# Moving two score pieces, their transposes and the U sums of each later batch in a fused attention and mixer kernel

## The chip, the cores and the metric

The kernel runs on one core of one Trainium2 chip. Its time is the device time of one execution in microseconds; before the change the median of three runs is 314.85 us (314.42 to 315.06). A core has a matrix engine (TensorE, PE), a vector engine (VectorE, DVE), a scalar engine (ScalarE, ACT), a general engine (GpSimd, POOL) and a sync engine (SyncE, SP). Each runs its own list of instructions in order; semaphores tie the lists together. DMA queues move data between HBM and the on-chip memory.

## The reference

Sliding window attention over 8 batches of 8 heads, 576 positions and head size 64, followed by a mixer: a low rank mix over positions (U and V, rank 32) with a residual, then two dense layers with a relu and a residual.

```python
scores = scale * np.matmul(q, k.transpose(0, 1, 3, 2))
rel = pos[:, None] - pos[None, :]
mask = (rel >= 0) & (rel < 64)
scores = np.where(mask, scores, -1000000000.0)
attn = softmax(scores)
x = np.matmul(attn, v)                  # heads side by side: (8, 576, 512)
h = x.transpose(0, 2, 1) @ U @ V        # mixes the 576 positions, rank 32
u = x + h.transpose(0, 2, 1)
ch = np.maximum(u @ w_ch1, 0.0) @ w_ch2 # 512 -> 2048 -> 512
out = u + ch
```

The line with softmax stands for the subtraction of the maximum, the exponential and the division by the sum.

## The kernel before

The 4608 rows (8 batches of 576) pass through the dense layers in nine chunks of 512. The loop over c at L927 writes one chunk: 32 slots with a last one for what is left, and in each slot four big matmuls. Slots 0 to 15 make psA from w1b and uT (L749), a block of 128 hidden units each, and a relu on ACT (L760) or DVE (L758, the numbers in DVE_RELU) writes it to c1. Slots 16 to 31 make psU from c1 and w2b (L793), four slots for each of four row tiles, and DVE adds u to it and sends it out (L808, L811). psA and psU share a pool of three PSUM buffers ("mm"). Two larger buffers ("big") serve scores, values and the V sums; one more bank ("tp") serves two small uses, the last head's values (xr8, L477) and a piece of the V sums (psv0, L549).

While chunk c runs, the attention of batch b = c + 1 is fitted into its slots. The order is written out by hand: the tables PLACE (batches 3 to 7), PLACE_1 and PLACE_2 give for each piece the slot after whose matmuls it is issued. Every engine receives its instructions in that order; there is no scheduler that moves them later. The pieces of a batch are:

- KT (L238): the transposes of k and q on DVE (L253), eight of them, k and q by turns. One of them reads all 128 partitions of the raw k or q and writes a quarter of kt or qt. kt and qt exist once, the raw tiles twice (by the parity of the batch).
- S (L353): five score pieces. PE writes sc (L378), ACT takes the exponential into pts (L386), DVE multiplies by the mask (L393). Piece n covers blocks 8n to 8n + 7 of 36, nine blocks to a pair of heads, so that the first two pieces need the first four transposes. pts exists once.
- VC (L140): two copies on DVE (L143, L144) that lay the values out a second time in vB.
- PV (L473, PVH at L450): the values, on PE; DVE divides by the sums and writes xs and xh.
- U (L517): the sums with U, pshh (L529), which ACT copies to hh (L538).
- V (L543): the sums with V, psv (L562), from hh.
- ADD (L572) and TR (L682): DVE adds xs to psv and so makes u (un), and transposes it into a staging tile stg.
- gather (L705): 16 small DMAs from the queues of SP, ACT and POOL that bring the staging tile into uT, the input of the next chunk.

The transposes of batch b + 1 are fitted into chunk c too, in the slots of KT_LATE. The loads of k and q (L117, four of each, each for 32 partitions) come from the POOL queue: in chunk c, one slot after the slot of V plus the gather, next_loads (L694) copies two elements of the gathered uT on POOL (hold, L698) and then issues the loads of batch c + 3. The values of batch b + 1 are loaded at the start of chunk c (L129, L135). Batches 2 and 3 are loaded earlier, in chunk 0.

Of the kernel before, what the change touches and what calls it, by code (L numbers as in the profile page):

```python
# [12 lines left out]
FP32 = mybir.dt.float32  # L13
# [3 lines left out]
def kernel(  # L17
# [12 lines left out]
    B, H, S, D = q.shape  # L30
# [3 lines left out]
    P = nc.NUM_PARTITIONS  # L34
# [12 lines left out]
    CH = 512  # L47
# [3 lines left out]
    HD = DM // 2  # L51
# [15 lines left out]
    ps_big = ctx.enter_context(tc.tile_pool(name="ps_big", bufs=2, space=bass.MemoryType.PSUM))  # L67
    first = ExitStack()
    psum = {
        "x0": first.enter_context(tc.tile_pool(name="ps_x0", bufs=2, space=bass.MemoryType.PSUM)),  # L70
    }
# [30 lines left out]
    def load_kq(b):  # L102
        r = RUN[b]
        for part in range(NJ if PAIRED[b] else 4):
            for x, src in (("k", k), ("q", q)):
                dst = raw[x, b % 2]
                if PAIRED[b]:
                    nc.gpsimd.dma_start(
                        out=dst[:, part * RD : (part + 1) * RD],
                        in_=src[b, part * NQ : (part + 1) * NQ].rearrange(  # L110
                            "i (p c) d -> (i p) (c d)", c=RP
                        ),
                    )
                    continue
                m, dh = divmod(part, 2)
                off = 32 * (1 - dh)
                nc.gpsimd.dma_start(  # L117
                    out=dst[32 * part : 32 * (part + 1), off : off + NJJ * RD].rearrange(
                        "p (n x) -> p n x", x=r * D
                    ),  # L120
                    in_=src[b, m * NJJ : (m + 1) * NJJ].rearrange(
                        "h (m p e) d -> p (h m) (e d)", p=32, e=r
                    ),
                )

    def load_v(b, first=True, second=True):
        va, vb = vA[b % 2], vB[b % 2]
        for t in range(0 if first else 2, NFULL if second else 2):
            nc.gpsimd.dma_start(  # L129
                out=va[:, t, :, 0:D],  # L130
                in_=v[b, :, t * P : (t + 1) * P, :].rearrange("h p d -> p h d"),
            )
        if not second:
            return
        nc.gpsimd.dma_start(  # L135
            out=vb[0:W, NFULL, :, 0:D],
            in_=v[b, :, NFULL * P : S, :].rearrange("h p d -> p h d"),
        )
# [90 lines left out]
    def attention(b, alone=False):  # L229
# [283 lines left out]
        hh = hh_of.setdefault(b, {})  # L513
# [3 lines left out]
        def UM(ts):  # L517
            def f():
                if ts[0] == 0:
                    big = ps_big.tile([P, 2, CH], FP32, name="pshh", tag="big")  # L520
                    hh["ps"] = big[:, 0, 0:HD]
                ps = hh["ps"]
                tops = (ub[0][:, NT - 1, :], ubh[0][:]) if not odd else (ubh[1][:], ub[1][:, 0, :])
                for t in [t for t in full if t in ts] + [t for t in ts if t == half_t]:
                    xt = (xh[odd] if t == half_t else x[:, t]).rearrange("p h d -> p (h d)")
                    n_th = 0 if t == half_t else full.index(t)
                    for n in range(2):
                        g = 2 * n + n_th % 2
                        nc.tensor.matmul(  # L529
                            ps[g * R : (g + 1) * R, :],  # L530
                            tops[n] if t == half_t else ub[odd][:, t, :],
                            xt if t == half_t else xt[:, n * HD : (n + 1) * HD],
                            start=(t != half_t and n_th < 2),
                            stop=(t == half_t or n_th == NFULL - 1),
                        )
                if ts[-1] == NT - 1:
                    hh["sb"] = wk_pool.tile([P, HD], BF16, name="hh", tag="hh")
                    nc.scalar.copy(out=hh["sb"][:], in_=ps)  # L538
            return f
# [135 lines left out]
        return pcs  # L675


    DVE_RELU = (1, 4, 7, 10, 13)
    stages = {}
    last_pieces = {}  # L680

    def TR(g):  # L682
        def f():
            c, t = divmod(g, TPC)
            if c not in stages:
                stages[c] = stg_pool.tile([P, 4 * NDC, TPC, 32], BF16, name="stg")
            nc.vector.transpose(  # L687
                out=stages[c][:, :, t, :],
                in_=u_tiles[g].rearrange("p (j x) -> p j x", x=32),
            )  # L690

        return f

    def next_loads(c):  # L694
        def f():
            for i, j in last_pieces[c + 1]:
                rows = slice(32 * j, 32 * (j + 1))
                nc.gpsimd.tensor_copy(  # L698
                    out=hold[rows, 0:1], in_=uT_of(c + 1)[rows, 0, i * TPC * 32 : i * TPC * 32 + 1]
                )  # L700
            load_kq(c + 3)

        return f
# [21 lines left out]
    def mlp(c):  # L725
# [11 lines left out]
        def ch1(i):  # L737
            def f():
# [17 lines left out]
                c1[i] = c1_pool.tile([P, CH], BF16, name=f"c1_{i}")  # L756
                if i in (DVE_RELU if c > 1 else (7, 10, 13) if c else (1, 5, 14)):
                    nc.vector.tensor_relu(out=c1[i][:], in_=ps)  # L758
# [59 lines left out]


    PLACE = {  # L820
        "VC": [2],
        "S": [0, 0, 4, 4, 9],
        "PV": [9, 12, 12],
        "KT": [14, 15, 16, 19, 21, 23, 25, 27],
        "U": [15],
        "V": [17],
    }
    PLACE_1 = {
# [13 lines left out]
        "S": [3, 3, 6, 6, 9, 9],  # L842
        "VC": [7],
        "PV": [12, 14, 14],
        "U": [17],
        "V": [18],
    }
    KT_LATE = {b: [21, 22, 23, 24, 25, 27, 28, 30] for b in range(2, B - 1)}


    def turn_over(n, cols=CH, to=None):
# [15 lines left out]
    att = {0: attention(0, alone=True)}  # L867
# [59 lines left out]
    for c in range(NCH):  # L927
        slots = [[] for _ in range(NSLOT + 1)]

        def place(b, parts, where):  # L930
            if b not in att:
                att[b] = attention(b)
            for part in parts:
                for f, s in zip(att[b][part], where[part]):
                    slots[s].append(f)

        b = c + 1
        if b == 1:
            slots[4].append(att[0]["V"][0])
            for f, n in zip(att[0]["ADD"], (5, 6, 7, 8, 4)):  # L940
                slots[n].append(f)
        if b < B:
            if b == 1:
                load_kq(2)
            if b + 1 < B:
                load_v(b + 1)
            if b == 1:
                slots[23].append(lambda: load_kq(3))
            where = {1: PLACE_1, 2: PLACE_2}.get(b, PLACE)
            if b == 2:  # L950
                place(1, ("V", "ADD"), {"V": where["V1"][:1], "ADD": where["ADD1"][:4]})
            if b == 1:
                place(1, ("KT",), where)
            if b == 2:
                att[2]["KT"] = att[2]["KT"][2:]
                place(2, ("KT",), where)
            place(b, ("VC", "S", "PV"), where)
            if b == 2:
                slots[where["V1"][1]].append(att[1]["V"][1])
                slots[where["ADD1"][4]].append(att[1]["ADD"][4])  # L960
            if b == 1:
                place(2, ("KT",), {"KT": PLACE_2["KT0"]})
            if 3 <= b + 1 < B:
                place(b + 1, ("KT",), {"KT": KT_LATE[b]} if b in KT_LATE else PLACE)
            place(b, ("U", "XT", "UP") if b == 1 else ("U", "V"), where)
        if 2 <= c + 1 < NCH:
            g0 = (b * S) // P
            first = (c + 1) * TPC
            own = [first + t - g0 for t in range(TPC) if b < B and first + t >= g0]
            at = where["V"][0] if b < B else 18  # L970
            for t in range(TPC - len(own)):
                slots[at - 1].append(TR(first + t))
            for n, t in enumerate(own):
                slots[at + n // 2].append(att[b]["ADD"][t])
                slots[at + n // 2].append(TR(g0 + t))
            ready = at
            slots[ready + 1].append(gather(c + 1))
            for n, t in enumerate(t for t in range(NT) if b < B and t not in own):
                slots[ready + 1 + n].append(att[b]["ADD"][t])
            if c > 0 and c + 3 < B:  # L980
                slots[ready + 1].append(next_loads(c))
        for n, (fill, extra) in enumerate(zip(mlp(c) + [lambda: None], slots)):
            early = c == 0 and n > 20
            for f in extra + [fill] if early else [fill] + extra:
                f()
# [30 lines left out]
```

## Time and profile before

| | |
|---|---|
| median of three runs | 314.85 us |
| profiled execution, its own time | 316.53 us |
| its span, from first to last instruction | 314.8 us |
| mean granted TensorE clock | 0.989 |
| chunk 4, from first psA to first psA | 159.46 to 191.65 us, 32.19 us |
| chunks 7 and 8, without attention | psA 13.81 us, psU 13.81 us for 64 matmuls each |
| k and q loads of a batch | eight of 288 KB read, median 10.9 and 12.0 us to landing |
| DMA packets under 512 B | 98544 of 109121 |

The page gives busy time by engine, the same in 40 slices of the span, the chain of work that ended last, and the costliest groups of instructions. The views asked of the trace beside it are the chain in order of time, the timeline of one engine, the instructions of one tile with the time that their DMAs took to land, and the busy time by stretches. A slice is 7.87 us; a digit is the busy share in tenths.

### The profile page before, as it was taken

How to read it: one execution, taken by the hardware profiler on the slowest of the kernel's cores; microseconds unless marked ns; L12 is line 12 of the kernel's file. 1: busy time of each engine (PE TensorE's matmuls, PEld its weight loads, DVE VectorE, ACT ScalarE, POOL GpSimd, SP SyncE). 2: the span in 40 equal slices, each digit the busy share in tenths (PEclk: the TensorE clock that was granted, in tenths of full speed). 3: DMA queues.
4: the chain of work that ended last, by engine and by line, in shares of the span. 5: the costliest groups of instructions: out<-in, count | busy, mean ns of one | idle time of the engine just before them, and what ended most of it. 6: DMA issues, size and time to landing. Idle time of an engine off the chain costs nothing.

```text
span 314.8 us, 7156 instructions
## 1 busy us (share of the span) xinstructions
PE 306.6 (97%) x2959; PEld 150.7 (48%) x2959; DVE 205.5 (65%) x371; ACT 105.7 (34%) x173; POOL 109.1 (35%) x162
## 2 busy tenths in 40 slices
PE   8799999998999999999999999999999999999995
PEld 7454455454444544454444444544444444444444
DVE  6655863897798679767966796689668622413111
ACT  1444752484107410551056204630463014103400
POOL 8591466482049404740583039303000300300000
PEclk9969999999999999999999999999999999999999
DMA  6999999999959995999599959995100510230011
GB/s 115 158 158 211 192 181 196 104 154 230 68 133 169 175 101 134 161 176 109 135 177 177 91 127 147 195 112 134 70 2 2 130 70 0 59 109 34 3 67 67
DMA packets 109121, 38.06 MB, mean 121 GB/s; under 512 B 98544, under 2 KB 102000, under 8 KB 109088
## 3 DMA queue, kind: packets, MB, share of 16 engines
q0 software_dynamic: 92672, 25.64, 113.6%
q1 hardware_dynamic: 11232, 10.69, 10.8%
q10 hardware_dynamic: 5184, 1.28, 2.2%
q8 instruction: 23, 0.38, 0.6%
q14 instruction: 10, 0.08, 0.1%
HBM read 48.96 MB, written 9.44 MB: 185 GB/s over the span
## 4 chain that ended last, share of the span: by engine, by line
PE 87%; DMA 6%; DVE 3%; ACT 2%; issue 1%; POOL 0%; DVEq 0%; POOLq 0%
PE psA L749 38%; PE psU L793 36%; PE sc L378 3%; DMA vB<-in_v_dram 3%; DMA qr<-in_q_dram 3%; PE xr L485 2%; PE psv L562 1%; PE psU L773 1%; PE pshh L529 1%; PE xr L417 1%; ACT pts L386 1%; DVE qt L245 1%; PE xT L626 1%; ACT pts L336 0%; PE xrh L457 0%
## 5 line engine op out<-in xcount | busy, mean ns | idle before, releaser
L749 PE MATMUL psA<-uTc,w1b 128*128 128x512 bf16 x576 | 131.0, 380 | 0.0
L793 PE MATMUL psU<-w2b,c 128*128 128x512 bf16 x560 | 125.0, 380 | 0.0
L760 ACT ACTIVATE c<-psA 128x512 bf16<-128x512 f32 x103 | 61.0, 599 | 161.8 <-PE psA L749 148.2
L749 PEld LDWEIGHTS <-w1b 128*128 128x128 bf16 x576 | 54.0, 98 | 63.6 <-issue 1.5
L793 PEld LDWEIGHTS <-c 128*128 128x128 bf16 x560 | 53.2, 98 | 64.8 <-issue 3.3
L713 POOL DMA_DIRECT2D uTc<-stg x35 | 19.2, 558 | 101.5 <-DVE stg L687 30.3
L758 DVE TENSOR_SCALAR c<-psA 128x512 bf16<-128x512 f32 x41 | 28.2, 687 | 19.8 <-PE psA L749 18.0
L808 DVE TENSOR_TENSOR osb<-psU,un 128x512 f32<-128x512 f32 x33 | 22.3, 675 | 28.7 <-PE psU L793 28.5
L393 DVE TENSOR_TENSOR pts<-pts,mask 128x1024 bf16<-128x1024 bf16 (+2 forms) x37 | 23.8, 654 | 24.4 <-ACT pts L386 23.6
L129 POOL DMA_DIRECT2D vA<-in_v_dram x32 | 28.8, 902 | 25.3 <-PE psA L749 12.4
L386 ACT ACTIVATE pts<-sc 128x1024 bf16<-128x1024 f32 (+2 forms) x37 | 31.5, 895 | 5.6 <-PE sc L378 5.6
L580 DVE TENSOR_TENSOR un<-psv,xs 128x512 bf16<-128x512 f32 x29 | 19.0, 675 | 4.7 <-PE psv L562 4.6
L687 DVE STREAM_TRANSPOSE stg<-un 128x512 bf16<-128x512 bf16 x28 | 18.8, 695 | 0.4
L117 POOL DMA_DIRECT2D kr<-in_k_dram x20 | 16.4, 820 | 5.3 <-DMA vA<-in_v_dram 2.7
L117 POOL DMA_DIRECT2D qr<-in_q_dram x20 | 16.5, 827 | 2.8 <-DMA vA<-in_v_dram 2.2
L253 DVE STREAM_TRANSPOSE kt<-kr 128x576 bf16<-128x576 bf16 x20 | 15.8, 788 | 0.1
L253 DVE STREAM_TRANSPOSE qt<-qr 128x576 bf16<-128x576 bf16 x20 | 15.7, 783 | 0.0
L378 PEld LDWEIGHTS <-kt 64*64 64x64 bf16 (+1 forms) x720 | 10.3, 106 | 10.0 <-issue 9.6
L378 PE MATMUL sc<-qt,kt 64*64 64x128 bf16 (+4 forms) x720 | 13.3, 215 | 0.9 <-issue 0.7
L499 DVE TENSOR_TENSOR xs<-xr,rcp 128x896 bf16<-128x896 f32 x12 | 13.1, 1092 | 0.1
L593 DVE TENSOR_TENSOR un<-psv,xh 64x256 bf16<-64x256 f32 x16 | 6.7, 417 | 6.7 <-PE psv L562 6.5
L853 PE MATMUL unread<-idle 128*128 128x64 bf16 (+2 forms) x108 | 7.5, 244 | 1.3 <-DVE idle L147 1.3
(93 smaller groups left out, 195.1 us busy)
## 6 DMA issues: line engine op xcount, KB each, us to landing
out_dram<-osb SPq DMA_DIRECT2D x35, 256.0 KB, 2.2
kr<-in_k_dram POOLq DMA_DIRECT2D x26, 288.0 KB, 10.9
qr<-in_q_dram POOLq DMA_DIRECT2D x26, 288.0 KB, 12.0
vA<-in_v_dram POOLq DMA_DIRECT2D x32, 128.0 KB, 12.6
w2b<-in_moe_w_ch_dram POOLq DMA_DIRECT2D x4, 512.0 KB, 12.6
uTc<-stg SPq DMA_DIRECT2D x42, 32.0 KB, 2.3
uTc<-stg ACTq DMA_DIRECT2D x35, 32.0 KB, 2.3
uTc<-stg POOLq DMA_DIRECT2D x35, 32.0 KB, 2.1
```

The costliest lines, as they stand in the source:

```text
L117: nc.gpsimd.dma_start(out=dst[32 * part : 32 * (part + 1), off : off + NJJ * RD].rearrange("p (n x) -> p n x", x=r * D), in_=src[b, m * NJ ...
L129: nc.gpsimd.dma_start(out=va[:, t, :, 0:D], in_=v[b, :, t * P : (t + 1) * P, :].rearrange("h p d -> p h d"),)
L253: nc.vector.transpose(out=dst[:, n * S : (n + 1) * S].rearrange("q (m p e) -> q m e p", p=32, e=r), in_=src[:, 32 + n * RD : 32 + (n + 1) ...
L378: nc.tensor.matmul(sc[half * W : (half + 1) * W, g, (a - lo) * W : (z - lo) * W], operand("k", g, jj, e, kb * W, (kb + 1) * W), operand("q ...
L386: nc.scalar.activation(out=dst, in_=sc[:, :, 0 : (hi - lo) * W].rearrange("p g (n w) -> p g n w", w=W), func=ACT.Exp, scale=scale,)
L393: nc.vector.tensor_tensor(out=dst, in0=dst, in1=mask[:, m0 : m0 + hi - lo, :] .unsqueeze(1) .to_broadcast([P, 2, hi - lo, W]), op=ALU.mult,)
L713: queues[n % 3].dma_start(out=uT_of(c)[32 * j : 32 * (j + 1), :, i * run : (i + 1) * run], in_=stages[c][32 * i : 32 * (i + 1)].rearrange( ...
L749: nc.tensor.matmul(to if c < 2 else to.rearrange("p (t i q) -> p t i q", i=4, t=TPC), w1b[:, dc, n * P : (n + 1) * P], uT_cols(dc), start= ...
L758: nc.vector.tensor_relu(out=c1[i][:], in_=ps)
L760: nc.scalar.activation(out=c1[i][:], in_=ps, func=ACT.Relu)
L793: nc.tensor.matmul(acc[t][:], c1[i][:, t * P : (t + 1) * P], w2b[:, i, :], start=(i == 0), stop=(i == NFC - 1),)
L808: nc.vector.tensor_tensor(out=osb[:], in0=acc[t][:], in1=u_tiles[g][:], op=ALU.add)
```

## The change

The first two score pieces of batches 3 to 7 are issued a chunk sooner, after the U sums of the preceding batch and in their slot; the other three pieces, the values and the U sums move to earlier slots. For the early pieces, the first four transposes of batches 4 to 7 move to slots 9 to 12 and those of batch 3 to slots 15 to 17; the other four follow from slot 21 on (25 for batch 3). The second layout of the values (VC) moves to slot 31 of the chunk before. The U sums of batches 2 to 7 take the bank "tp" in place of a "big" buffer. In chunk 1 the U sums of batch 2 stand at slot 19 and not 17, its V sums at slot 22 and not 18, and with them the gather and the loads that follow. Three of the five relus on DVE change their number. No instruction is added or removed.

```diff
--- before.py
+++ after.py
@@ -517,8 +517,10 @@
         def UM(ts):
             def f():
                 if ts[0] == 0:
-                    big = ps_big.tile([P, 2, CH], FP32, name="pshh", tag="big")
-                    hh["ps"] = big[:, 0, 0:HD]
+                    if b < 2:
+                        hh["ps"] = ps_big.tile([P, 2, CH], FP32, name="pshh", tag="big")[:, 0, 0:HD]
+                    else:
+                        hh["ps"] = psum["tp"].tile([P, CH], FP32, name="pshh", tag="tp")[:, 0:HD]
                 ps = hh["ps"]
                 tops = (ub[0][:, NT - 1, :], ubh[0][:]) if not odd else (ubh[1][:], ub[1][:, 0, :])
                 for t in [t for t in full if t in ts] + [t for t in ts if t == half_t]:
@@ -675,7 +677,7 @@
         return pcs
 
 
-    DVE_RELU = (1, 4, 7, 10, 13)
+    DVE_RELU = (1, 2, 5, 10, 13)
     stages = {}
     last_pieces = {}
 
@@ -818,11 +820,9 @@
 
 
     PLACE = {
-        "VC": [2],
-        "S": [0, 0, 4, 4, 9],
-        "PV": [9, 12, 12],
-        "KT": [14, 15, 16, 19, 21, 23, 25, 27],
-        "U": [15],
+        "S": [0, 0, 4],
+        "PV": [4, 7, 7],
+        "U": [14],
         "V": [17],
     }
     PLACE_1 = {
@@ -842,10 +842,13 @@
         "S": [3, 3, 6, 6, 9, 9],
         "VC": [7],
         "PV": [12, 14, 14],
-        "U": [17],
-        "V": [18],
+        "U": [19],
+        "V": [22],
     }
-    KT_LATE = {b: [21, 22, 23, 24, 25, 27, 28, 30] for b in range(2, B - 1)}
+    KT_EARLY = {b: [9, 10, 11, 12] for b in range(4, B)}
+    KT_EARLY[3] = [15, 15, 16, 17]
+    KT_LATE = {b: [21, 23, 25, 27] for b in range(4, B)}
+    KT_LATE[3] = [25, 27, 29, 30]
 
 
     def turn_over(n, cols=CH, to=None):
@@ -954,15 +957,20 @@
             if b == 2:
                 att[2]["KT"] = att[2]["KT"][2:]
                 place(2, ("KT",), where)
-            place(b, ("VC", "S", "PV"), where)
+            if b >= 3:
+                att[b]["S"] = att[b]["S"][2:]
+            place(b, ("S", "PV") if b >= 3 else ("VC", "S", "PV"), where)
             if b == 2:
                 slots[where["V1"][1]].append(att[1]["V"][1])
                 slots[where["ADD1"][4]].append(att[1]["ADD"][4])
             if b == 1:
                 place(2, ("KT",), {"KT": PLACE_2["KT0"]})
             if 3 <= b + 1 < B:
-                place(b + 1, ("KT",), {"KT": KT_LATE[b]} if b in KT_LATE else PLACE)
+                place(b + 1, ("KT",), {"KT": KT_EARLY[b + 1] + KT_LATE[b + 1]})
+                place(b + 1, ("VC",), {"VC": [31]})
             place(b, ("U", "XT", "UP") if b == 1 else ("U", "V"), where)
+            if 3 <= b + 1 < B:
+                place(b + 1, ("S",), {"S": where["U"] * 2})
         if 2 <= c + 1 < NCH:
             g0 = (b * S) // P
             first = (c + 1) * TPC
```

## The prediction

> **What bounds the kernel now.** I read the busy shares first, then the chain of waits, and last the timelines of the DVE and POOL around one batch. The page shows a TensorE that hardly pauses:
>
> ```profile
> PE 306.6 (97%) x2959; PEld 150.7 (48%) x2959; DVE 205.5 (65%) x371; ACT 105.7 (34%) x173; POOL 109.1 (35%) x162
> PE   8799999998999999999999999999999999999995
> PEclk9969999999999999999999999999999999999999
> DMA  6999999999959995999599959995100510230011
> ```
>
> The DMA row matters as much: until slice 28 the queues are full, apart from one dip per batch. The chain of waits confirms PE, and gives the cost of each piece in one steady chunk (start us, length, what):
>
> ```profile
> 159.46 0.86 PE psA L749 x4
> 160.32 0.57 PE sc L378 x32
> 160.89 3.61 PE psA L749 x16
> ...
> 173.84 2.70 PE psA L749 x12
> 176.53 0.43 PE pshh L529 x10
> 176.97 1.83 PE psU L793 x8
> 178.80 0.65 PE psv L562 x10
> 179.45 12.19 PE psU L793 x56
> 191.65 0.86 PE psA L749 x4
> ```
>
> Start to start this chunk (c=4) takes 191.65 - 159.46 = 32.19 us; one slot, four matmuls, is 0.86. The PE does the same work after the change, so a gain can only come from gaps, and there are few. What can go wrong is a wait, so I looked at what the moved pieces wait for. In the POOL timeline of chunk 2's end the loads of batch 5's k and q follow the gather of the next uT and the "hold" copies that read it; in the DVE timeline its transposes come in chunk 3:
>
> ```profile
> 124.81 0.42 POOL L698 COPY hold<-uTc 32x1 bf16<-32x1 bf16 x2 [2.39 <-DMA uTc<-stg]
> 125.40 0.83 POOL L117 DMA_DIRECT2D kr<-in_k_dram  x1 [0.17 <-issue]
> 131.03 0.83 POOL L117 DMA_DIRECT2D qr<-in_q_dram  x1
> ```
>
> ```profile
> 152.29 0.82 DVE L253 STREAM_TRANSPOSE kt<-kr 128x576 bf16<-128x576 bf16 x1
> 153.02 0.77 DVE L253 STREAM_TRANSPOSE qt<-qr 128x576 bf16<-128x576 bf16 x1
> ```
>
> The view by tile, cut to 124-132 us, gives for the four q loads (least, median, most):
>
> ```profile
> DMA to landing us min/median/max: 9.8/13.4/16.4
> ```
>
> 16.4 is the last one's, so batch 5's q is whole at 131.03 + 16.4 = 147.4. Each transpose (L253) reads all 128 partitions, and one load fills only 32 of them: every transpose, the first too, needs all four loads. Chunk 3 starts at 127.27; q lands 20.2 us into it, 4.9 us before its first transpose now.
>
> [...] So a transpose that waits holds up every relu behind it. The trace agrees in that DVE's order is the program's. [...] The windows view of the start agrees (us, then busy us of PE, PEld, DVE, ACT, POOL, granted clock, DMA, GB/s):
>
> ```profile
> 8.02:11.43 3.41, 2.79 (x61) 1.77 (x60) 1.62 (x2) 1.51 (x2) 2.44 (x4) 1.00 1.88 168
> 11.43:14.84 3.41, 2.08 (x126) 1.73 (x124) 3.17 (x7) 1.38 (x2) 1.46 (x3) 1.00 2.30 138
> 14.84:18.25 3.41, 3.09 (x42) 1.85 (x42) 1.66 (x5) 2.15 (x6) 2.52 (x5) 0.50 1.30 136
> 18.25:21.67 3.42, 3.42 (x43) 1.80 (x43) 2.37 (x6) 1.25 (x7) 3.42 (x7) 0.50 1.16 170
> ```
>
> A stretch of 3.41 us with PE busy for 2.08 was followed by two at half clock; one with 2.79 was not. [...] The trace agrees: twelve matmuls between two switches take 2.70, against 13.81/64 x 12 = 2.59 in the unbroken stretches at the end, so 0.11 per group.
>
> **The change part by part.**
>
> Small things first. The relus: five stay on DVE, other numbers; 0.69 on DVE against 0.60 on ACT, all beside matmuls: 0. The U sums in the "tp" bank: its last user, xr8, is read by slot 7, and the next, psv0, comes three slots after the 0.37 us copy of hh: 0. The V copies (0.68 + 0.70) at slot 31 of the chunk before: their last load is issued at 142.56, lands after a median 9.7, 152.3, before slot 31 (about 158): 0, and if late they would hold a DVE that has only an output sum to do. The two early score pieces keep their cost of 0.57 but ride behind the U sums, so a group disappears per batch: -0.11 five times, and the last attention chunk is 0.57 shorter, paid a chunk sooner.
>
> The transposes carry the price. The first four (k, q, k, q) of batches 4 to 7 move from slots 21-24 to 9-12 of the same chunk; the loads don't move forward. In the new order DVE has, after slot 9: k transpose, relu 10, q, k, q, relu 13, then the two masks. The psA pool has three buffers: with relu 10 held, PE stops at the matmuls of slot 13, about 13 x 0.86 + 2.2 of scores and values = 13.4 us into the chunk; with the q transposes held, the scores at slot 14 stop. Landing is at 17.4 to 20.2 us. ACT's exp and hh copy are queued behind PE, and the loads of the next batch behind this chunk's values (V, slot 17), so the delay comes again each chunk.
>
> So I follow one loop, from the V matmuls (psv) of a chunk to those of the next: psv to first k issue; first k issue to last q landing; then three transposes (0.7 + 0.7 + 0.77 = 2.2), two score pieces 0.57, three slots 2.70, together 5.47. Measured now:
> batch 4: psv 82.75, issue 94.27, q whole 99.90 + 14.5 = 114.4, so 11.52 + 20.13;
> batch 5: psv 114.15, 125.40, 147.4: 11.25 + 22.03;
> batch 6: 146.61, 155.98, 161.64 + 15.2 = 176.84: 9.37 + 20.86;
> batch 7: 178.80, 189.09, 194.72 + 15.8 = 210.52: 10.29 + 21.43.
>
> Chunk 1 first. Batch 3's last q load (issued 64.55, 18.3 to land) is whole at 82.85, its k at 80.34. Transposes now stand at slots 15-17, so the fourth ends at 85.05; PE has done slot 19 and the U sums (79.62 + 3.45 + 0.43) at 83.5 and waits 1.55. Scores 0.57 and three slots 2.70: psv at 88.35, where it was 82.75. The gather moves along (V at slot 22, not 18): uT lands 10.6 after psv, 99.0, but only 8.4 us of PE work follow, so chunk 2 starts 2.2 late; that lies inside the next wait.
>
> Then psv of chunk 2: 88.35 + 31.65 + 5.47 = 125.47; chunk 3: + 33.28 + 5.47 = 164.22; chunk 4: + 30.23 + 5.47 = 199.92; chunk 5: + 31.72 + 5.47 = 237.11. Before it was 210.99: +26.1, and less 0.68 in chunk 6: +25.4. The loops are 37.1, 38.8, 35.7, 37.2 us against 32.2 of PE work: PE idles 3.5 to 6.5 us in each.
>
> Unknown is the clock after such a stop. By the windows above, more than 1.33 us idle in one of them can halve it; each of the four stops would. [...] Half of that is lost, less 0.65 that PE would have waited for q anyway: 1.05 to 2.75, I take 1.9. What is slow behind psv costs nothing: PE waits for loads there. Below zero it can't go; at zero the masks and uT transposes behind the late scores would cost up to 1.0 in its place. Four times 1.9 is 7.6.
>
> Sum: 25.4 + 7.6 = +33.0 on the span of 314.8: 347.8, and 1.7 around it in the profiled execution (316.53). The median of the runs, 314.85, lies 1.7 below that execution; 314.85 + 33.0 = 347.9, taken as 348.
>
> **Rivals.** (a) The same loop with the clock full: +25.4, and up to 1.0 for three of the DVE's late masks, about 341. For it: stretches with small matmuls may be judged otherwise than these. Against: the start's half-clock stretch. (b) The late load is paid once: if the later loads ran ahead of PE, only chunk 2's share (125.47 - 114.15 = 11.3) would stay: 326. Against: the hold copies that tie the loads to uT. (c) The half clock lasts over the whole way from resumption to psv, about 6 us of work each time: 25.4 + 4 x 5.4 = +47, 362. (d) No stop: were q whole by 13.4 us into a chunk, the price of the transposes would be 0 and the saved switches (5 x 0.11) and chunk 2's small stop (its chunk is 32.54, not 32.19) would show: -0.9, 313.9. It decides only if landing shrinks by 4.0 us or more; the four measured landings span 1.9.
>
> **How the numbers follow.** Forecast 0.64; (a) 0.17; (b) 0.07; (c) 0.08; (d) 0.04. Landing may differ by a microsecond in each of four loops, and the clock by 0.85 each, so the forecast's own range is 341 to 355; (a) and part of (c) widen it to 334 to 358. No change means within 0.2%, what a measurement of this kernel can tell. (d) splits into faster 0.03 and same 0.01; the rest, 0.96, is slower.
>
> **What would show it.** DVE timeline: a gap before the k transpose in chunks 2 to 5, ended by kr or qr; PE gaps before psA of slot 13 and sc of slot 14; chunks of 36 to 40 us; PEclk of 0.5 after each. Were the gaps at uT or psv, or the transposes on time, the loop is wrong.

## The result and the profile after

The changed kernel takes 344.99 us (median of four runs, 344.35 to 347.11) against 314.73 for the kernel before on the same chip: a ratio of 1.0973 with a 95% interval of 1.0922 to 1.1024. (Single executions that the chip disturbed are left out, here and below; where a run gives one time only, that is why.) The profiled execution took 344.48 us, its span is 342.8 us, 28.0 more than before.

The first lines to compare are the same four of the page:

```profile
PE 312.7 (91%) x2930; PEld 154.4 (45%) x2959; DVE 205.3 (60%) x371; ACT 107.4 (31%) x173; POOL 110.6 (32%) x162
...
PE   8779999999979599995999799986999999999995
...
PEclk9999999999989879998999989998999999999999
DMA  7999999999299905999399907999510050051012
```

PE no longer runs through: there are dips four to five slices (a chunk) apart, the granted clock dips with them, and the DMA row, which was full, now has empty slices. The work is the same, so neither engine has more to do; both stand still by turns. The chain of waits says who waits for whom. This is chunk 2's end and chunk 3 (start us, length, what):

```profile
135.66 0.18 POOL hold L700
135.84 0.17 issue
136.01 0.83 POOL kr L117
...
142.09 14.37 DMA qr<-in_q_dram
...
156.65 0.82 DVE qt L253
157.47 0.67 DVE kt L253
158.14 0.68 DVE qt L253
...
158.86 0.51 PE sc L378 x9
159.38 1.84 PE psA L751 x4
...
161.43 2.15 PE psU L795 x7
163.58 0.34 PE psv L564 x4
163.93 0.02 issue
163.95 0.70 DVE un L582
164.67 0.71 DVE stg L689
```

Before, the chain ran through PE alone in such a chunk. Now it is a ring: the hold copies, the eight loads, the landing of the last q, three transposes, the scores, three slots of PE, the V sums, and the tiles that make the next uT, whose arrival lets the next loads go. DMA has 24% of the chain and PE 49%, where they had 6% and 87%.

The DVE timeline of the same chunk shows the wait itself (the bracket is the idle time ahead of the instruction, and what ended it):

```profile
154.30 0.82 DVE L253 STREAM_TRANSPOSE kt<-kr 128x576 bf16<-128x576 bf16 x1 [4.38 <-DMA kr<-in_k_dram]
155.02 0.65 DVE L760 TENSOR_SCALAR c<-psA 128x512 bf16<-128x512 f32 x1
156.65 0.82 DVE L253 STREAM_TRANSPOSE qt<-qr 128x576 bf16<-128x576 bf16 x1 [0.98 <-DMA qr<-in_q_dram]
157.37 0.77 DVE L253 STREAM_TRANSPOSE kt<-kr 128x576 bf16<-128x576 bf16 x1
158.04 0.77 DVE L253 STREAM_TRANSPOSE qt<-qr 128x576 bf16<-128x576 bf16 x1
```

and the PE timeline shows where it arrives:

```profile
147.85 6.26 PE L751 MATMUL psA<-uTc,w1b 128*128 128x512 bf16 x28
154.04 0.40 PE L531 MATMUL pshh<-xs,ub 128*32 128x256 bf16 x8
...
157.52 0.45 PE L378 MATMUL sc<-qt,kt 64*64 64x128 bf16 x20 [2.97 <-DVE qt L253]
158.86 0.53 PE L378 MATMUL sc<-qt,kt 64*64 64x128 bf16 x14 [0.89 <-DVE qt L253]
...
163.51 0.72 PE L564 MATMUL psv<-hh,vrep 64*128 64x256 bf16 x10
```

Two things are to be seen. Slots 8 to 14 (28 matmuls) run without a break although relu 10, at 155.02, comes later: PE does not stop at slot 13. It stops at the early scores, 2.97 and 0.89 us, the second time within the second piece, which needs the fourth transpose.

From V to V the loops are 124.53 - 86.05 = 38.48, then 38.98, 36.52 and 38.78 us (V at 86.05, 124.53, 163.51, 200.03, 238.81), against 31.5 and three times about 32.3 before.

### The profile page after: what moved, and what is told of

Its sections match the earlier page's. It is cut to its first block, busy times and chain, and to the rows that moved or that the text cites. A ratio compares the mean times of both kernels' runs of the same rounds, so it can differ in the third digit from the quotient of the medians.

```text
span 342.8 us, 7129 instructions
## 1 busy us (share of the span) xinstructions
PE 312.7 (91%) x2930; PEld 154.4 (45%) x2959; DVE 205.3 (60%) x371; ACT 107.4 (31%) x173; POOL 110.6 (32%) x162
## 4 chain that ended last, share of the span: by engine, by line
PE 49%; DMA 24%; DVE 9%; POOL 8%; issue 3%; SPq 3%; ACT 2%; ACTq 0%; DVEq 0%; POOLq 0%
PE psU L795 22%; PE psA L751 20%; DMA qr<-in_q_dram 19%; POOL kr L117 4%; DMA uTc<-stg 3%; POOL qr L117 3%; SPq L715 3%; DMA vrep<-in_moe_V_dram 2%; DVE stg L689 2%; PE sc L378 2%; DVE qt L253 2%; ACT pts L386 2%; DVE un L582 2%; PE psv L564 1%; PE psU L775 1%
## 5 line engine op out<-in xcount | busy, mean ns | idle before, releaser
L751 PE MATMUL psA<-uTc,w1b 128*128 128x512 bf16 x568 | 134.8, 387 | 5.5 <-DMA uTc<-stg 2.5
L795 PE MATMUL psU<-w2b,c 128*128 128x512 bf16 x540 | 126.3, 387 | 2.2 <-issue 1.5
L795 PEld LDWEIGHTS <-c 128*128 128x128 bf16 x560 | 54.9, 100 | 68.4 <-issue 8.4
L760 DVE TENSOR_SCALAR c<-psA 128x512 bf16<-128x512 f32 x41 | 27.4, 679 | 21.4 <-PE psA L751 19.9
L378 PE MATMUL sc<-qt,kt 64*64 64x128 bf16 (+5 forms) x720 | 15.0, 223 | 13.9 <-DVE qt L253 13.1
L378 PEld LDWEIGHTS <-kt 64*64 64x64 bf16 (+1 forms) x720 | 12.2, 110 | 22.3 <-issue 17.4
L117 POOL DMA_DIRECT2D qr<-in_q_dram x20 | 17.4, 870 | 3.0 <-DMA vA<-in_v_dram 2.4
L499 DVE TENSOR_TENSOR xs<-xr,rcp 128x896 bf16<-128x896 f32 x12 | 13.1, 1092 | 0.1
```

The source lines that it names most:

```text
L117: nc.gpsimd.dma_start(out=dst[32 * part : 32 * (part + 1), off : off + NJJ * RD].rearrange("p (n x) -> p n x", x=r * D), in_=src[b, m * NJ ...
L378: nc.tensor.matmul(sc[half * W : (half + 1) * W, g, (a - lo) * W : (z - lo) * W], operand("k", g, jj, e, kb * W, (kb + 1) * W), operand("q ...
L751: nc.tensor.matmul(to if c < 2 else to.rearrange("p (t i q) -> p t i q", i=4, t=TPC), w1b[:, dc, n * P : (n + 1) * P], uT_cols(dc), start= ...
L795: nc.tensor.matmul(acc[t][:], c1[i][:, t * P : (t + 1) * P], w2b[:, i, :], start=(i == 0), stop=(i == NFC - 1),)
```

## Experiments

Each run is compared with the kernel before on its chip. The theories are named in what was expected of the runs. Line numbers are those of each kernel; the edits are against the changed kernel where nothing else is said.

**No wait for the loads.**

```diff
+    spare = {x: const.tile([P, NJJ * RD + 32], BF16, name=f"{x}s") for x in "kq"}
...
-                dst = raw[x, b % 2]
+                dst = raw[x, b % 2] if b < 4 else spare[x]
...
-            src, dst = raw[x, odd], trs[x]
+            src, dst = raw[x, odd if b < 4 else 1], trs[x]
```

> The changed kernel, but the loads of k and q of batches 4 to 7 go to a spare tile (the same transfers at the same places) and the transposes of these batches read batch 3's k and q, so that no transpose waits for a load; the scores of batches 4 to 7 are therefore those of batch 3. Theory A (the early transposes wait for their loads, and the wait comes again in each chunk): no stop is left, 313 to 317 us, chunks 3 to 5 of about 32 us, clock never at half after 25 us. Rival B (the other moves cost the time: U sums in the tp bank, scores behind the U sums, relus renumbered, gather later in chunk 1): 330 us or more.

Measured: 322.89 us, ratio 1.025 (1.021 to 1.0289). The long stops are gone, so three quarters of the loss are the wait for the loads; the scores, U sums and values at their new places don't explain it. But 8 us stay, more than the theory allowed. The waits of PE, longest in total first (total, times, longest), name most of them:

```profile
PE psA L752 <- DVE c L761: 3.2, 5, 0.6
PE psA L752 <- DMA uTc<-stg: 2.5, 1, 2.5
PE sc L379 <- DVE qt L254: 2.0, 2, 1.1
```

The first is new to the prediction: psA of slot 4 waits for a relu on DVE in each of five chunks. The second is chunk 2's late uT, the third the early scores of batch 3, whose loads this edit leaves in use.

**Relus 10 and 13 off the DVE.**

```diff
-    DVE_RELU = (1, 2, 5, 10, 13)
+    DVE_RELU = (1, 2, 5)
```

> The changed kernel with relus 10 and 13 on ACT, so that no relu stands behind a waiting transpose. Theory A: PE passes slot 13, stops at the early scores instead, and the loop from V to V is bound by the landing of q all the same: 342 to 350 us. Rival B (the relus queued behind the transposes are what costs): the stop at slot 13, about 4 us in each of four chunks, goes: 325 to 332 us.

Measured: 344.34 us, one time alone. No gain is seen: the scores on PE hold the loop, whether or not relus stand behind the waiting transposes. In this the expectation was met, but not for the reason given: PE had not stopped at slot 13 in the changed kernel either.

**Something for PE to do in the stop.** (In the loop over the slots, before the slot's own matmuls.)

```diff
+    FILL = 18
...
+            if 2 <= c <= 5 and n == 13:
+                still = psum["tp"].tile([P, CH], FP32, name="still", tag="tp")
+                for _ in range(FILL):
+                    nc.tensor.matmul(still[:], idle[:, 0:P], idle[:], start=True, stop=True)
```

> The changed kernel with 18 idle matmuls of 128x512 (3.9 us at full clock) before slot 13 in chunks 2 to 5, where PE stands still. Nothing of them is read. Theory A with its clock part: the clock stays full and each loop is shorter by what the half clock cost, 1.5 to 2.5 us: 335 to 340 us. Rival C (the half clock costs nothing, the loop is bound by loads alone): 344 to 346. Rival D (PE is the bound there): 3.9 us more in four chunks, about 360.

Measured: 340.88 us (338.32 to 342.79), just above the range of the theory; ratio 1.087 (1.0819 to 1.0921), whose interval ends where that of the changed kernel begins. All three times lie below the lowest of the changed kernel, 344.35, but they spread over 4.5 us; the profiles are clearer. Views by stretches of 3.4 us, first the changed kernel, then this run (us, then busy us of PE, PEld, DVE, ACT, POOL, granted clock, DMA, GB/s):

```profile
114.80:118.20 3.40, 0.54 (x22) 0.53 (x21) 2.97 (x5) 0.92 (x3) 0.00 (x0) 0.97 4.19 132
118.20:121.60 3.40, 2.61 (x19) 1.32 (x21) 2.79 (x5) 2.06 (x3) 0.00 (x0) 0.50 0.64 20
```

```profile
114.80:118.20 3.40, 2.10 (x36) 1.13 (x35) 2.43 (x5) 1.67 (x3) 0.00 (x0) 1.00 3.12 99
118.20:121.60 3.40, 3.33 (x32) 1.63 (x33) 2.48 (x5) 1.82 (x3) 0.00 (x0) 1.00 0.05 5
```

With 18 matmuls more per stop the clock is 1.00 throughout this profile. From the landing of the last q to the V sums the changed kernel takes 8.09, 7.02, 7.00 and 6.76 us in its four loops, this run 5.29, 5.47, 5.53 and 5.24: on average 7.22 against 5.38. So the half clock costs 1.8 us per stop on average. The idle matmuls cost next to nothing: in chunks 3 and 4 of this run no early score waits any more, so PE is the last to come there, yet the way from the landing is at most 0.3 us longer than in chunks 2 and 5.

**Scores late, transposes early.**

```diff
-                place(b + 1, ("S",), {"S": where["U"] * 2})
+                place(b + 1, ("S",), {"S": [29, 29] if b > 2 else where["U"] * 2})
```

> The changed kernel with the first two scores of batches 4 to 7 at slot 29 and not behind the U sums; their transposes stay at slots 9 to 12. Theory A: relus 10 and 13 still stand behind the waiting transposes and hold slots 13 and 16, so the loop is at most 1 us shorter: 338 to 345 us. Rival E (the scores that wait on PE are what costs): 314 to 322 us.

Measured: 331.93 us in the middle of two times (329.84 and 334.02), ratio 1.0537 (1.045 to 1.0623): less than expected, between the two theories, and neither held. DVE still waits for k, but PE feels it only in small stops. In chunk 4 they are

```profile
185.64 1.02 PE L751 MATMUL psA<-uTc,w1b 128*128 128x512 bf16 x4 [0.31 <-ACT c L762]
187.41 1.89 PE L795 MATMUL psU<-w2b,c 128*128 128x512 bf16 x8 [0.74 <-ACT c L762]
```

and they end with relus on ACT, not on DVE: with one buffer held by a waiting relu, PE goes on with the others. The clock is 1.00 from 182.0 to 192.2 us, also in and after the stretch with the two stops, where PE is busy for 2.42 of 3.40 us. Some two fifths of the loss, 13.1 of 30.3 us, thus hang on the early scores alone. Of what stays, some 8 us are what the run without waits kept as well. The profiled span exceeds that of the run without waits by 6.7 us, and the two small stops shown, 1.05 us together in each of four chunks, are 4.2 of it: once the scores no longer hold the loop, relus behind waiting transposes do cost something.

**Loads sooner.** The loads of batches 4 to 7 at slot 8 of chunk 1 and slot 2 of chunks 2 to 4; the gather from two queues; no hold copies.

```diff
-            queues = (nc.sync, nc.scalar, nc.gpsimd)
+            queues = (nc.sync, nc.scalar)
...
-                slots[ready + 1].append(next_loads(c))
+                slots[8 if c == 1 else 2].append(next_loads(c))
```

> The changed kernel with the loads of k and q of batches 4 to 7 issued some 15 slots sooner (slot 8 of chunk 1, slot 2 of chunks 2 to 4, not behind the gather), without the hold copies, and the gather from the queues of SP and ACT alone. Nothing is left out. Theory A: the transposes find their data and the long stops go; what the run without waits kept (8 us) stays, and the gather may be slower beside full queues: 320 to 328 us. Rival (the loads can't come sooner since the queues are full, so the wait only moves to uT or to the values): 335 us or more.

Measured: 343.15 us, ratio 1.0907 (1.0849 to 1.0965): the rival held. No early score of batches 4 to 7 waits for a transpose any more, but chunk 2 starts 17 us late (the profile names an output's DMA as the last to come, but what the matmul reads is uT):

```profile
112.86 1.87 PE L744 MATMUL psA<-uTc,w1b 128*128 128x512 bf16 x4 [17.36 <-DMA out_dram<-osb]
```

The gather of uT, with the loads in the queues beside it, takes three times as long to land, 7.1 us in the median and not 2.3. View by tile, uTc, first the changed kernel in chunk 1, then this run (least, median, most):

```profile
DMA to landing us min/median/max: 1.9/2.3/2.7
```

```profile
DMA to landing us min/median/max: 5.4/7.1/9.8
```

and where the changed kernel issues its six pieces on SP between 91.2 and 94.7, this run issues eight between 92.0 and 102.7. The gather has two queues here and not three; at the pace of the changed kernel, (94.7 - 91.2) / 5 = 0.7 us apiece, that alone would make the issue some 1.4 us longer by estimate, not 7, but its share in the landing was not tested. In chunks 4 and 5, once the backlog of chunk 1 is past, the loops of this run are 32.8 us: there the loads come in time and uT too. So in chunk 1 the wait has only moved from the loads to uT.

**The small stops.** Two runs on top of the one without waits. First the relus:

```diff
-    DVE_RELU = (1, 2, 5, 10, 13)
+    DVE_RELU = (1, 4, 7, 10, 13)
```

> The run without waits (322.9 us; batches 4 to 7 take batch 3's k and q), with the relus on DVE numbered as before the change, 1, 4, 7, 10, 13. Theory F (psA of slot 4 waits 0.63 us in each of five chunks for a relu that stands behind two masks): 3.2 us less, 319 to 320.5. Rival (that gap is only shown there, and PE would wait for the exponentials or masks anyway): 322 to 323.5.

Measured: 320.96 us (320.25 to 322.96), 1.9 less in the median; one of the four times is as long as those without the edit (322.68 and 323.1), so the profile decides. It has none of the five 0.63 us gaps; between the V sums of chunks 3 and 6 it takes 248.07 - 152.40 = 95.67 us, where the run without waits took 249.70 - 151.78 = 97.92. Its batch 3 waited longer this time (1.6 and 0.9 us at the scores, against 1.1 and 0.9), which hides part of the gain.

Then U and V of chunk 1 as well:

```diff
-        "U": [19],
-        "V": [22],
+        "U": [17],
+        "V": [18],
...
-                place(b + 1, ("S",), {"S": where["U"] * 2})
+                place(b + 1, ("S",), {"S": [21, 21] if b == 2 else where["U"] * 2})
```

> As the run before, and in chunk 1 U at slot 17, V at slot 18, with the two early scores of batch 3 in a group of their own at slot 21 (batches 4 to 7 still take batch 3's k and q). Theory F: uT is in time for chunk 2, and the early scores of batch 3 wait no more: 2.5 for uT and about 1.5 for the scores less, 314.5 to 316.5, which is the time before. Rival (something else of the change costs, such as the tp bank or the values a slot sooner): 318 or more.

Measured: 322.29 us (319.77 to 323.88), no further gain. uT is in time, but the scores of batch 3 now stop for something else:

```profile
88.29 0.42 PE L379 MATMUL sc<-qt,kt 64*64 64x64 bf16 x18 [2.82 <-DVE un L583]
```

They need a "big" buffer, and the V sums of slot 18 hold both until DVE has added them up; behind this stop the next 39 psU matmuls take 10.27 us, 1.9 more than at the 13.81 / 64 us apiece of chunks 7 and 8. Slot 21 was a bad choice; that uT's 2.5 us were won is seen in the profile, not in the time.

**Loads sooner, with both small repairs.** The edits of the last three runs together, with the loads in use.

> The loads issued sooner as in the first of these four, with the relus and U and V of chunk 1 as in the third. Nothing is left out. Theory A and F together: 313 to 318 us, as before the change or a little better. Rival (full queues slow the gather or the values): 322 or more.

Measured: 336.56 us (335.35 to 339.81), ratio 1.0685 (1.0656 to 1.0713): again the rival. The two findings before, the gather behind the loads and the scores behind the V sums, let one expect a loss; how much of it each of them makes was not taken apart.

**Transposes and scores behind the landing.** All transposes from slot 21, the first two scores a chunk sooner still, but at slot 30; relus, U and V of chunk 1 as before the change; the rest of the change stays.

```diff
-    KT_EARLY = {b: [9, 10, 11, 12] for b in range(4, B)}
-    KT_EARLY[3] = [15, 15, 16, 17]
-    KT_LATE = {b: [21, 23, 25, 27] for b in range(4, B)}
-    KT_LATE[3] = [25, 27, 29, 30]
+    KT_EARLY = {b: [9, 10, 11, 12] for b in range(8, B)}
+    KT_LATE = {b: [21, 23, 25, 27] for b in range(8, B)}
+    for b in range(3, 8):
+        KT_EARLY[b], KT_LATE[b] = [21, 22, 23, 24], [25, 26, 27, 28]
...
-                place(b + 1, ("S",), {"S": where["U"] * 2})
+                place(b + 1, ("S",), {"S": where["U"] * 2 if b + 1 >= 8 else [30, 30]})
```

(B is 8, so both ranges from 8 are empty.)

> The changed kernel with only the early transposes and scores put back behind the landing: all transposes of batches 3 to 7 from slot 21 on, their first two scores still a chunk sooner, but at slot 30; relus and U and V of chunk 1 as before the change. Values and U sums stay sooner, the U sums in the tp bank, the values' second layout at slot 31. Nothing is left out. Theory A and F: nothing waits, 313.5 to 316 us, which is the time before. Rival (the tp bank, the sooner values or the copies at slot 31 cost): 317 or more.

Measured: 315.05 us against 315.26, ratio 0.9996 (0.9978 to 1.0014). That is the time before, within what can be told. The "tp" bank, the sooner values and U sums and the copies at slot 31 together cost nothing and bring nothing; the two scores at slot 30 are a group of their own, so no group of small matmuls is saved here. The page has its PE row unbroken again:

```profile
PE   8779999999999999999999999999999999999995
```

**Two batches early.** As the last run, but batches 6 and 7 as in the changed kernel (slots 9 to 12, scores behind the U sums).

> As the run before, but batches 6 and 7 have their early transposes at slots 9 to 12 and their scores behind the U sums, as in the changed kernel; so two chunks, 4 and 5, have the stop. Nothing is left out. Theory A (each chunk pays anew, since the loads follow its V sums): two loops of 4 to 7 us more, 323 to 329. Rival (b) of the prediction (the late load is paid once): one stop, 319 to 321.

Measured: 326.95 us, ratio 1.0362 (1.0314 to 1.0411): 11.7 us more than before for two batches. The scores stop in both chunks, the second time no less:

```profile
178.02 0.45 PE L378 MATMUL sc<-qt,kt 64*64 64x128 bf16 x20 [1.71 <-DVE qt L253]
...
215.85 0.69 PE L378 MATMUL sc<-qt,kt 64*64 64x128 bf16 x20 [4.54 <-DVE qt L253]
```

The loops that end with the V sums of these two chunks are 182.38 - 146.72 = 35.66 and 222.58 - 182.38 = 40.20 us, against 32.19 before. So each early batch pays anew, as the ring says, though not the same; a load that is late once and then caught up is ruled out.

No run beats the kernel before. The saving looked for, one group of small matmuls fewer per batch (0.11 us, five times), is below what the times can tell, but a profile shows it. In the first run of the small stops, where no transpose of batches 4 to 7 waits, the V sums of chunks 3 to 6 stand at 152.40, 184.48, 216.56 and 248.07: loops of 32.08, 32.08 and 31.51 us, where each of the three was 32.19 before. That is the 0.11 us per chunk and the 0.68 us in chunk 6 that the prediction forecast; why a group costs 0.11 us beside its own matmuls is not shown.

## Why the prediction was right, point by point

The time of 344.99 lies in the range, 3 us under the forecast, and the cause forecast is the one the runs show: the transposes wait for loads that did not move (the run without waits), the early scores carry that to PE (the late scores, and the run with transposes and scores behind the landing), and it comes again per batch (two batches early).

- **The loop** was the right sum. Its terms, forecast and measured, added over the four loops: V to first issue 42.4 and 43.8 us; first issue to last landing 84.5 and 80.1; landing to V at full clock 21.9 and, taken from the run with idle matmuls, 21.5; half clock 7.6 and 7.3. Landing was the term that was too large: the loads were whole 18.6 to 20.9 us after the first issue, not 20.1 to 22.0 (why they landed sooner is not shown). The forecast of the span, 347.8, exceeds 342.8 by 5.0 us. Landing makes 4.4 of it, chunk 1 (next point) 2.3, the way from landing to V with its clock 0.6; against these, V to first issue took 1.4 more than forecast, and the way from the last of these V sums to the end 0.9. So the forecast is close in part because errors offset each other.
- **Chunk 1** was forecast to wait 1.55 us for batch 3's loads. In the profiled run its four transposes ran from 79.58 to 82.47 without a wait, and the V sums stood at 86.05, not 88.35. Other runs, such as the first one of the small stops, did wait there. The 2.2 us for uT came as 2.55, and as forecast lay inside the next wait.
- **The stop at slot 13 was wrong.** The step said that with relu 10 held PE stops there, since the pool has three buffers. PE passed slots 13 and 14 in all four chunks and stopped only at the scores behind them. With one buffer held by the waiting relu PE went on with two: in chunk 3 the 28 matmuls of slots 8 to 14 took 6.26 us from 147.85, and relu 10 began at 155.02. The sum did not suffer, since it counts from the landing of q, and the scores behind the q transposes set the loop either way; but an edit of the relus, which this step suggests, gained nothing.
- **The relus at zero were wrong.** Relu 1 stands behind two masks on DVE as before, but with relu 2 on DVE too psA of slot 4 gets the buffer that relu 1 still holds: 0.63 us in each of five chunks in the run without waits (3.2 together), in chunks 3 to 6 here. In the changed kernel this lies inside the waits for the loads, except in chunk 6, where it eats the 0.68 us forecast as a gain: from the V sums of chunk 5 to the end it took 104.0 us, and 103.9 before.
- **DVE's order and the clock.** Relu 10 does stand behind the k transpose: in the DVE timeline of chunk 3 that transpose begins at 154.30 after an idle time of 4.38 us, and the relu only at 155.02. It cost less than argued. The clock was 0.50 after each of the four stops, which was worth 1.8 us each on average, forecast 1.9. The forecast's length of the half clock, 5.1 us, was the author's estimate, between one and two stretches of 3.41 us; the start of the kernel before had shown two, 14.84 to 21.67. That each stop would bring it was taken from one stretch of that start, with PE busy for 2.08 of 3.41 us. It came true, but the busy time of a stretch does not decide it, as the last section shows.
- **Rivals.** (a), a full clock, falls by the PEclk row and the idle matmuls; (b), once only, by the two batches; (c), a longer half clock, since it lasted one stretch of 3.4 us after three of the stops, two after the other; (d) would have needed the loads 4 us sooner. Moving them, in the way tried, cost at uT in chunk 1 about what it saved (343.15 us in all).

## What to carry to other kernels

Before a consumer is moved forward, find when its data land, relative to the slot and not to the consumer's present place: here 5 us of slack stood against a move of 12 slots. If the load is issued after something that the delayed work produces, the loss is not a single stall but a longer period, paid in every turn (36.5 to 39.0 us here, 32.2 before). And look at what stands beside a load that is moved earlier: here the pieces of uT took 7.1 us to land beside the moved loads, and 2.3 without them (with two queues for the gather in the one case and three in the other).

## What the hardware showed unexpectedly

Two short stops were enough for a half clock. In chunk 4 of the changed kernel PE stood only 0.80 and 0.89 us:

```profile
193.10:196.50 3.40, 1.70 (x40) 1.19 (x39) 3.31 (x5) 2.35 (x4) 0.00 (x0) 1.00 2.95 94
196.50:199.90 3.40, 3.18 (x8) 1.02 (x7) 1.91 (x3) 0.90 (x2) 0.00 (x0) 0.50 0.01 2
```

PE was busy for half of the stretch, 1.70 of 3.40 us, and the next one ran at 0.50. (The stretches in this section start at a change of the clock in that execution, or a whole number of 3.41 us stretches from one. In the changed kernel the clock changes at 97.5, 100.9, 118.0, 124.8, 159.0, 162.4, 196.5, 199.9, 234.1 and 237.5 us.) In the first run of the small stops a stretch with PE busy for less, 1.48 us, was followed by full clock:

```profile
98.77:102.18 3.41, 1.48 (x40) 0.83 (x40) 2.58 (x5) 0.36 (x1) 1.92 (x3) 1.00 0.62 197
102.18:105.60 3.42, 3.42 (x26) 1.48 (x16) 1.98 (x3) 3.15 (x5) 3.42 (x6) 1.00 1.12 109
```

So the busy time of PE, as these profiles give it, does not tell whether the clock will be halved; what else counts is not shown.

Small transfers landed later beside large ones that had been issued on another engine's queue: the pieces of uT, 32 KB each beside loads of 288 KB, took 2.3 us to land in the changed kernel, where the k and q loads follow them, and 7.1 us in the run with the loads sooner, where these stood before and beside them (and the gather had two queues, not three).
